# An attention and gated feed-forward block: a written-out opening, query heads parted by DMA, and a planner whose clocks wait for copies

## The chip, the cores and the metric

The kernel runs on one core of one Trainium2 chip. The metric is device time in microseconds (us). Nine runs of the kernel before lie between 734.39 and 735.54 us, with a median of 735.0 us.

The engines have short names in the profile: PE (TensorE matmul), PEld (TensorE weight load), DVE (VectorE), ACT (ScalarE), POOL (GpSimd) and SP (SyncE, which here only issues DMAs).

## What is computed

A block of a transformer over 2048 tokens of 512 features, with 32 heads of 16 features and a gated feed-forward part of 1792 features. All tensors are bfloat16.

```python
def _A_ref(x, wqkv, wo):
    qkv = (x @ wqkv).reshape(B, S, 3, H, Dh).transpose(2, 0, 3, 1, 4)
    q, k, v = qkv[0], qkv[1], qkv[2]
    scores = jnp.einsum("bhqd,bhkd->bhqk", q, k) * (Dh ** -0.5)
    o = jnp.einsum("bhqk,bhkd->bhqd", softmax(scores), v)
    return o.transpose(0, 2, 1, 3).reshape(B, S, D) @ wo

def _B_ref(x, w_gate, w_up, w_down):
    return (sigmoid(x @ w_gate) * (x @ w_up)) @ w_down

h = x + _A_ref(layernorm(x), A_wqkv, A_wo)
h2 = h + _B_ref(layernorm(h), B_w_gate, B_w_up, B_w_down)
```

## The kernel before, in words

**The main loop.** Scores are made transposed, 128 keys by 512 query columns at a time, for one head: 2048 such units in all. PE multiplies a slice of keys `KT` with queries `QT` (line 1110, 32 of its rows for each head) into a tile of PSUM that holds two or three units. ACT takes the exponential of most units (line 1475, into `pt` and into other buffers that are free at that time, so the profile shows the names `pe`, `xb`, `xnT` and `QTb` as well). DVE makes the exponential of the remaining units with integer arithmetic on 16-bit words (line 1292, tile `J`): one instruction writes the word, and two "chords", the same word plus a constant, are made by POOL as 64-bit integer additions (line 1313) or, early on, by DVE (line 1319). The three are summed in the product with the values: three matmuls for each such unit where an ACT unit has one. In a variant that the plan chooses ("both" in the code), DVE first adds two of the three as half-precision tiles (line 1337), which leaves two matmuls. PE multiplies probabilities with the values `Vaug` (line 1268), which carry a 17th column of halves, so that the sum of the probabilities comes out beside the output.

**Queries in pairs of groups.** The features of a 128-row projection hold eight heads of 16 rows. PE's scores read 32 rows at a time, so each projection goes into two tiles, `QT[2p]` and `QT[2p+1]`: one has the even heads and zeros in the rows of the odd ones, the other the reverse. In `prep_q` DVE scales the projection into `qd` (line 778), and `split_q` (line 327) multiplies `qd` with a mask column, once for each of the two tiles. This happens 15 times, for four blocks of 512 queries and four feature blocks, the first of them in the opening. One of the 15 goes to `QTb`, half of the tile `QTB`.

**Order.** Nothing is scheduled by the hardware or by a compiler: the Python program decides the order on each engine as it emits instructions. It keeps a clock for each engine, `T["P"]`, `T["A"]`, `T["D"]`, `T["G"]`, adds a fixed cost for every instruction, and places background work (projections, layer norms, the feed-forward part of finished query blocks) where these clocks have room. Jobs for DVE wait in the list `dq`, in order of priority. `need` (line 1090) forces the key and query jobs of a score unit to have been emitted before the scores. A table `PLAN`, with a number for a step of a score tile, overrides single decisions: how many value matmuls follow, whether a unit goes to DVE, whether PE rests, and others.

**The opening (lines 229 to 514).** SP and ACT's queue load the first 512 tokens, SP then the weights for the first feature block (`w0`), the other tokens and weights. POOL and DVE build an identity matrix from a ramp. For each of four token tiles, DVE or ACT makes mean and variance (ACT for the second tile), ACT the root, DVE the reciprocal (line 427) and the normalised tile `xn` (line 388), PE four transposes (line 308), ACT or DVE a copy out of PSUM (line 395). PE then projects keys and queries of the first feature block (line 401), and copies (lines 406 and 415) write the first parts of `KT` and `QT`. The order comes from a greedy list scheduler at lines 478 to 512 that takes the task with the best key of start and rank, with fixed costs, and keeps PE busy with filler matmuls (line 475). The scores begin when both halves of the query and the first half of the keys are there (`"go"`). The halves column of `Vaug` is written by ACT (line 265), the mask by DVE (lines 269 and 271), the accumulator is zeroed by DVE (line 514).

**After the opening.** `early_ln` normalises the other 1536 tokens (DVE statistics, POOL the rest), in blocks 2 and 3 with DMA transposes issued by SP (line 593). `prep_v` makes the values: a copy and a scaled copy on DVE (lines 323 and 324). `early_k` makes further keys of the first feature block (line 757), `prep_k` those of the others (line 767). In the feed-forward part SP issues transposes of the normalised `hn` (line 837), weight loads `wgu` with two buffers (line 855), loads of `x` (line 795) and stores (line 873). A filler matmul on `wo_sb` (line 678) keeps PE busy where nothing is ready.

Of the kernel before, what the change touches and what calls it, by code (L numbers as in the profile page):

```python
# [22 lines left out]
PLAN = {176: 5, 239: 2, 367: 1, 383: 1, 414: 3, 432: 9, 480: 5, 492: 1, 496: 3, 512: 4, 561: 1, 592: 3, 593: 9, 606: 3, 609: 3, 736: 5, 751: 2, 780: 2, 785: 1, 796: 1, 800: 4, 831: 1, 844: 2, 849: 3, 894: 3, 897: 9, 914: 9, 928: 3, 960: 2, 976: 3, 1025: 2, 1040: 3, 1041: 5, 1052: 2, 1072: 3, 1088: 2, 1100: 2, 1104: 5, 1105: 3, 1120: 3, 1170: 1, 1233: 3, 1280: 3, 1328: 4, 1359: 2, 1392: 3, 1440: 2, 1486: 3, 1681: 1, 1824: 5, 1840: 9, 1872: 4, 1953: 3, 1982: 1, 2001: 3, 2080: 3, 2095: 2, 2129: 3, 2161: 3, 2162: 2, 2176: 4, 2222: 1, 2239: 2, 2256: 4, 2257: 9, 2274: 4, 2287: 2, 2350: 3, 2412: 1, 2430: 2, 2465: 9, 2479: 2, 2480: 9, 2512: 2, 2556: 2, 2560: 4, 2574: 2, 2588: 2, 2592: 5, 2608: 9, 2767: 1, 2818: 3, 2833: 9, 2849: 5, 2864: 3, 2908: 1, 2972: 2, 3020: 1, 3036: 1, 3056: 1, 3072: 3, 3169: 4, 3180: 2, 3184: 4, 3217: 2, 3234: 4, 3280: 4, 3360: 2, 3537: 2, 3617: 3, 3644: 2, 3681: 9, 3744: 3, 3756: 2, 3760: 3, 3820: 2, 3905: 4, 3938: 3, 3953: 3, 4066: 4, 4080: 3, 4081: 4, 4096: 2, 4112: 2, 4124: 1, 4129: 9, 4191: 2, 4204: 1, 4207: 2, 4225: 3, 4268: 2, 4284: 1, 4288: 2, 4337: 2, 4352: 3, 4398: 3, 4510: 2, 4526: 1, 4641: 4, 4700: 2, 4734: 3, 4737: 4, 4752: 9, 4754: 2, 4784: 4, 4802: 4, 4878: 3, 4880: 4, 4910: 2, 4924: 1, 4928: 1, 4930: 4, 5022: 2, 5058: 3, 5072: 4, 5090: 3, 5121: 4, 5164: 1, 5182: 3, 5185: 3, 5200: 3, 5201: 3, 5265: 4, 5280: 3, 5294: 1, 5308: 1, 5345: 2, 5359: 1, 5360: 9, 5378: 3, 5388: 1, 5424: 1, 5471: 1, 5488: 1, 5522: 2, 5553: 3, 5566: 3, 5600: 2, 5633: 4, 5650: 9, 5696: 2, 5712: 4, 5728: 4, 5742: 2, 5756: 2, 5760: 3, 5840: 2, 5906: 1, 5938: 3, 6082: 9, 6095: 2, 6096: 2, 6108: 2, 6140: 1, 6192: 3, 6194: 9, 6268: 1, 6274: 3, 6289: 4, 6319: 1, 6337: 5, 6384: 1, 6431: 2, 6432: 4, 6463: 2, 6464: 4, 6528: 3, 6544: 3, 6592: 1, 6607: 2, 6624: 1, 6641: 2, 6656: 2, 6687: 2, 6689: 9, 6753: 9, 6799: 1, 6832: 2, 6847: 2, 6865: 1, 6929: 2, 6972: 2, 6974: 1, 7024: 1, 7040: 3, 7106: 9, 7152: 5, 7154: 9, 7244: 2, 7248: 3, 7281: 3, 7296: 2, 7312: 1, 7376: 2, 7408: 9, 7410: 2, 7468: 1, 7504: 4, 7505: 2, 7520: 3, 7535: 2, 7553: 4, 7566: 3, 7570: 4, 7585: 3, 7596: 2, 7676: 1, 7681: 5, 7695: 2, 7728: 4, 7776: 3, 7793: 2, 7839: 2, 7852: 1, 7886: 2, 8016: 2, 8033: 2, 8063: 2, 8128: 2, 8209: 4, 8257: 9, 8290: 4, 8305: 9, 8338: 4, 8382: 2, 8432: 5, 8494: 3, 8529: 5, 8591: 2, 8609: 5, 8626: 2, 8706: 3, 8721: 4, 8768: 4, 8800: 4, 8848: 2, 8849: 5, 8860: 1, 8863: 2, 8881: 3, 8882: 4, 8895: 2, 8896: 3, 8897: 2, 8910: 3, 8927: 1, 8946: 4, 8961: 4, 9006: 1, 9024: 3, 9026: 9, 9054: 3, 9073: 2, 9116: 2, 9120: 3, 9137: 4, 9153: 2, 9249: 5, 9276: 2, 9358: 2, 9376: 3, 9377: 9, 9407: 1, 9408: 1, 9426: 9, 9457: 3, 9504: 2, 9518: 3, 9520: 4, 9584: 9, 9586: 4, 9600: 2, 9678: 1, 9697: 1, 9711: 2, 9727: 2, 9728: 1, 9762: 9, 9776: 4, 9792: 4, 9841: 9, 9854: 2, 9855: 2, 9857: 9, 9872: 3, 9900: 1, 9919: 2, 9932: 1, 9964: 2, 9968: 3, 10028: 2, 10032: 2, 10044: 2, 10047: 1, 10146: 2, 10160: 5, 10172: 1, 10176: 3, 10177: 3, 10210: 4, 10273: 4, 10284: 1, 10304: 3, 10334: 1, 10364: 2, 10380: 2, 10417: 9, 10433: 4, 10464: 1, 10556: 1, 10622: 1, 10624: 4, 10626: 9, 10636: 1, 10640: 4, 10690: 3, 10702: 2, 10705: 3, 10734: 3, 10754: 4, 10801: 3, 10802: 2, 10816: 2, 10848: 9, 10912: 1, 10913: 1}  # L23
# [121 lines left out]
def kernel(  # L145
# [11 lines left out]
    nc = tc.nc  # L157
# [89 lines left out]
    nc.sync.dma_start(out=wo_sb[:], in_=A_wo.rearrange("(c p) n -> p c n", p=P))  # L247
# [8 lines left out]
    for k in range(32):  # L256
        nc.gpsimd.memset(ramp[:, 0, k:k + 1], float(k))
    nc.vector.memset(ident_bf[:], 0.0)
# [5 lines left out]
    def halves():  # L264
        nc.scalar.activation(out=Vaug[:, :, :, DH:VW], in_=fill[:].rearrange("p (t h o) -> p t h o", t=NT, o=1),
                             func=ACT.Copy, scale=0.5)

    def masks():
        nc.vector.tensor_reduce(out=mask[:], in_=ident_bf[:].rearrange("p (b a d) -> p a b d", a=2, d=DH),
                                axis=AX.XY, op=ALU.max)  # L270
        nc.vector.tensor_scalar(out=maskz[:], in0=mask[:], scalar1=ZS, scalar2=None, op0=ALU.mult)

# [57 lines left out]
    psp = main.enter_context(tc.tile_pool(name="psum", bufs=1, space=PSUM))  # L330
    PS = psp.tile([P, 8, QC], FP32, name="PS")
    free_banks = [5, 7, 6, 3, 2, 1, 0]
    held_banks = {}

    def bank0(key):
        b = held_banks[key] = free_banks.pop()
        return PS[:, b, :]

    def free0(key):
        free_banks.append(held_banks.pop(key))  # L340
# [7 lines left out]
    class Task:  # L348
        def __init__(self, name, deps, opts, bank=0, frees=0):
            self.name, self.deps, self.opts, self.bank, self.frees = name, deps, opts, bank, frees  # L350
            self.end = None
            tasks[name] = self

    def fixed(name, at):
        Task(name, [], []).end = at

    V, A, E = nc.vector, nc.scalar, nc.tensor

    ACT_STATS = {(0, 1)}

    def stats_task(c, i):
        src, mv = xb[c][:, i, :], mvs[c][:, i, :]

        def on_act():
            junk = work.tile([P, D], BF16, name="junk")
            A.activation(out=junk[:], in_=src, func=ACT.Identity, scale=1.0 / D,
                         accum_out=mv[:, 0:1])
            A.activation(out=junk[:], in_=src, func=ACT.Square, scale=D ** -0.5,
                         accum_out=mv[:, 1:2])
            buf["fix", c, i] = True  # L370
        Task(("s", c, i), [("x", c, i)], [("A", 1650, on_act)] if (c, i) in ACT_STATS
             else [("D", 870, lambda: ln_stats(src, mv))])
        Task(("f", c, i), [("s", c, i)], [("D", 300, lambda: fix(c, i))] if (c, i) in ACT_STATS
             else [("N", 0, lambda: None)])
# [19 lines left out]
    def copy0(c, i, eng):  # L394
        eng(out=xnv[c][:, i], in_=buf["t", c, i])
        free0(("t", i))
# [7 lines left out]
    def keys0(half, act):  # L404
        cs = slice(half * 2 * P, (half + 1) * 2 * P)
        (A.copy if act else V.tensor_copy)(out=KT[0][:, cs], in_=buf[0][:, cs])
        if half:
            free0(0)

    def query0(half, a, act=False):  # L410
        cs = slice(half * 2 * P, (half + 1) * 2 * P)
# [5 lines left out]
        if half and a:  # L417
            free0(1)

    fixed("w0", 5000.0)  # L420
    for c in range(NQC):
        for i in range(TQ):
            fixed(("x", c, i), (3150.0 + 450 * (i // 2)) if c == 0 else 4800.0 + 2100 * c + 150 * i)
            stats_task(c, i)
    for i in range(TQ):
        Task(("q", 0, i), [("f", 0, i)], [("A", 270, lambda i=i: root(i))])
        Task(("r", 0, i), [("q", 0, i)], [("D", 200, lambda i=i: V.reciprocal(
            out=rstds[0][:, i:i + 1], in_=rstds[0][:, i:i + 1]))])
        Task(("a", 0, i), [("r", 0, i)], [("D", 340, lambda i=i: apply(0, i))])
        Task(("t", 0, i), [("a", 0, i)], [("P", 400, lambda i=i: turn0(0, i))], bank=1)  # L430
        Task(("e", 0, i), [("t", 0, i)],
             [("A", 500, lambda i=i: copy0(0, i, A.copy)),
              ("D", 440, lambda i=i: copy0(0, i, V.tensor_copy))], frees=1)
        for w in (1, 0):
            Task(("p", w, i), [("e", 0, i), "w0"], [("P", 340, lambda w=w, i=i: proj0(w, i))], bank=int(i == 0))
    Task("mask", [("s", 0, 3)], [("D", 450, masks)])
    Task("halves", [("s", 0, 1)], [("A", 640, halves)])
    for h in range(2):
        for w in (1, 0):
            deps = [("p", w, 2 * h), ("p", w, 2 * h + 1)]  # L440
            if w:
                deps = deps + ["mask"]
                Task(("qt", h), deps, [("A", 450, lambda h=h: query0(h, 0, True)),
                                       ("D", 400, lambda h=h: query0(h, 0))])
                Task(("qu", h), deps, [("D", 400, lambda h=h: query0(h, 1))], frees=h)
            else:
                Task(("kt", h), deps, [("A", 410, lambda h=h: keys0(h, True)),
# [1261 lines left out]
```

## Time and profile before

| What | Value |
|---|---|
| median of nine runs | 735.0 us |
| the profiled execution | 734.96 us |
| its span | 733.2 us |
| DVE exponentials (line 1292) | 623, mean 679 ns |
| ACT exponentials into `pt` alone (line 1475) | 512, mean 1125 ns |
| sums of two tiles (line 1337) | 97, mean 702 ns |
| POOL chords (line 1313) | 658, mean 626 ns |
| projections of queries scaled, `qd` (line 778) | 15, mean 677 ns |
| granted TensorE clock | 0.999 of full speed |

A row of a timeline gives start and length in us, engine, line, operation, tile written and tile read, its shapes and the count, and in brackets how long the engine was idle before it and what ended that. A row of the waits gives who waited for whom, the total in us, how often and the longest. A group's row gives durations in ns as minimum, median and maximum. A busy engine is one with an instruction recorded on it; the records of neighbouring instructions overlap, so a short wait between two of them does not show as idle time.

### The profile page before, as it was taken

The numbers are of one execution on the slowest core, as the hardware profiler recorded it, in microseconds if no ns is written. First come the engines' busy times: TensorE is split into PE (matmuls) and PEld (weight loads), VectorE is DVE, ScalarE is ACT, GpSimd is POOL, SyncE is SP. The second block draws the span as 40 slices with busy tenths as digits, with TensorE's granted clock in tenths as the row PEclk, the third lists the DMA queues.
The fourth block names the chain that finished last, engine by engine and source line by source line (L and its number), as shares of the span: only waits on it lengthen the run. The fifth ranks groups of instructions, "written<-read, shape, count | busy, mean of one in ns | idle before, by whom it ended". The sixth has DMA issues, their size and how long they took to land.

```text
span 733.2 us, 26369 instructions
## 1 busy us (share of the span) xinstructions
PE 703.4 (96%) x11139; PEld 337.3 (46%) x11194; DVE 663.5 (90%) x1314; ACT 703.0 (96%) x787; POOL 421.7 (58%) x727
## 2 busy tenths in 40 slices
PE   7899999888999999999999999999999999999997
PEld 3222224443555445544545455445554455445564
DVE  6889999989999999999999899999999988999952
ACT  7999999999999999999999999999999999999962
POOL 2724667675665556656546656655654656656610
PEclk9999999999999999999999999999999999999999
DMA  7200005000223013220223023201322134012250
GB/s 244 51 9 2 1 1 175 2 3 2 74 75 88 10 27 101 84 56 25 59 67 86 20 69 101 66 25 31 101 61 52 38 89 117 17 44 80 84 175 18
DMA packets 80892, 44.49 MB, mean 61 GB/s; under 512 B 15488, under 2 KB 80768, under 8 KB 80768
## 3 DMA queue, kind: packets, MB, share of 16 engines
q1 hardware_dynamic: 80480, 42.48, 20.5%
q8 instruction: 89, 1.46, 0.9%
q14 instruction: 35, 0.29, 0.1%
q10 hardware_dynamic: 288, 0.26, 0.1%
HBM read 37.75 MB, written 2.10 MB: 54 GB/s over the span
## 4 chain that ended last, share of the span: by engine, by line
PE 48%; ACT 26%; DVE 18%; issue 4%; POOL 2%; DMA 1%; POOLq 0%; ACTq 0%; DVEq 0%
ACT pt L1475 18%; PE PS L1110 16%; PE PS L1268 13%; PE PS L847 8%; DVE J L1292 8%; PE PS L865 5%; ACT xnT L1475 3%; DVE J L1337 2%; POOL J L1313 2%; ACT th L877 2%; PE PS L319 1%; PE PS L314 1%; ACT QTb L1475 1%; DVE st L274 1%; ACT xb L1475 1%
## 5 line engine op out<-in xcount | busy, mean ns | idle before, releaser
L1313 POOL INT64_ADD J<-J x658 | 403.6, 626 | 260.9 <-DVE J L1292 211.2
L1475 ACT ACTIVATE pt<-PS 128x1024 f16<-128x1024 f32 (+1 forms) x512 | 512.9, 1125 | 3.9 <-PE PS L1110 2.8
L1292 DVE TENSOR_SCALAR J<-PS 128x512 int16<-128x512 f32 x623 | 411.4, 679 | 22.1 <-PE PS L1110 16.4
L1110 PE MATMUL PS<-QT,KT 32*128 32x256 bf16 (+1 forms) x3712 | 264.3, 276 | 15.0 <-ACT pt L1475 9.3
L1268 PE MATMUL PS<-J,Vaug 128*17 128x256 f16 (+1 forms) x3218 | 226.8, 279 | 0.9 <-DVE xs L1176 0.3
L1268 PE MATMUL PS<-pt,Vaug 128*17 128x256 f16 (+1 forms) x2021 | 191.8, 279 | 0.0
L1110 PEld LDWEIGHTS <-KT 32*128 32x128 bf16 x3840 | 90.3, 92 | 204.8 <-issue 201.2
L1268 PEld LDWEIGHTS <-Vaug 128*17 128x17 bf16 x5871 | 132.0, 90 | 79.8 <-issue 74.8
L847 PE MATMUL PS<-xnT,wgu 128*128 128x256 bf16 x784 | 112.5, 274 | 0.7 <-DVE qd L778 0.2
L1475 ACT ACTIVATE xnT<-PS 128x1024 f16<-128x1024 f32 (+1 forms) x88 | 96.1, 1128 | 0.0
L847 PEld LDWEIGHTS <-wgu 128*128 128x128 bf16 x784 | 64.4, 97 | 38.7 <-issue 33.0
L1337 DVE TENSOR_TENSOR J<-J 128x1024 f16<-128x1024 f16 (+1 forms) x97 | 67.9, 702 | 9.8 <-POOL J L1313 9.3
L865 PE MATMUL PS<-wd,hT 128*128 128x512 bf16 x169 | 51.0, 383 | 2.3 <-issue 2.2
L1268 PE MATMUL PS<-xnT,Vaug 128*17 128x256 f16 x360 | 51.8, 273 | 0.1
L877 ACT ACTIVATE th<-PS 128x512 f32<-128x512 f32 (+1 forms) x63 | 38.9, 618 | 8.4 <-DVE hT L860 5.6
L1475 ACT ACTIVATE QTb<-PS 128x1024 f16<-128x1024 f32 x39 | 43.1, 1105 | 0.3 <-PE PS L1110 0.3
L919 DVE SCALAR_TENSOR_TENSOR hT<-th,PS 128x512 bf16<-128x512 f32 x49 | 33.2, 678 | 2.8 <-PE PS L847 2.8
L1475 ACT ACTIVATE xb<-PS 128x1024 f16<-128x1024 f32 (+2 forms) x29 | 29.8, 1090 | 0.3 <-PE PS L1110 0.3
L1176 DVE STREAM_TRANSPOSE xs<-PS 128x256 f32<-128x256 f32 (+1 forms) x60 | 27.5, 458 | 1.8 <-PE PS L1268 1.6
L1475 ACT ACTIVATE pe<-PS 128x1024 f16<-128x1024 f32 (+2 forms) x26 | 25.9, 1059 | 1.7 <-PE PS L1110 1.6
L1268 PE MATMUL PS<-QTb,Vaug 128*17 128x256 f16 x156 | 27.1, 274 | 0.0
L1147 DVE TENSOR_TENSOR o<-xs,rsum 128x128 bf16<-128x128 f32 (+1 forms) x60 | 24.2, 404 | 2.1
(126 smaller groups left out, 394.0 us busy)
## 6 DMA issues: line engine op xcount, KB each, us to landing
wgu<-in_B_w_gate_dram SPq DMA_DIRECT2D x49, 256.0 KB, 3.0
wgu<-in_B_w_up_dram SPq DMA_DIRECT2D x49, 256.0 KB, 3.5
out_dram<-ob SPq DMA_DIRECT2D x16, 128.0 KB, 1.7
wd<-in_B_w_down_dram SPq DMA_DIRECT2D x1, 1792.0 KB, 8.8
xr<-in_A_x_dram SPq DMA_DIRECT2D x14, 128.0 KB, 3.5
xb<-in_A_x_dram SPq DMA_DIRECT2D x6, 256.0 KB, 6.0
J<-in_B_w_gate_dram SPq DMA_DIRECT2D x4, 384.0 KB, 5.3
J<-in_B_w_up_dram SPq DMA_DIRECT2D x4, 384.0 KB, 6.1
```

The costliest lines, as they stand in the source:

```text
L847: nc.tensor.matmul(ps[:, 0:PARTS[r][2]].rearrange("p (i q) -> p i q", q=P), lhsT=w[:, d, :], rhs=hn_of(r)[:, :, d, :], start=(d == 0), sto ...
L865: nc.tensor.matmul(ps, lhsT=hT[:, f, i * P:(i + 1) * P], rhs=wd[:, f, :], start=(f == 0), stop=(f == FC - 1))
L877: nc.scalar.activation(out=th[:, 0:ps.shape[-1]], in_=ps, func=ACT.Tanh, scale=0.5)
L919: nc.vector.scalar_tensor_tensor(out=hT[:, f:f + k, 0:w], in0=th[f][:].rearrange("p (k n) -> p k n", k=k), scalar=1.0, in1=ps2.rearrange(" ...
L1110: nc.tensor.matmul(pss[:, ui, i * CW[qc]:(i + 1) * CW[qc]], lhsT=KT[g // 2][32 * j:32 * j + 32, k * P:(k + 1) * P], rhs=q[32 * j:32 * j + ...
L1147: nc.vector.tensor_tensor(out=o2[:, 0:w // 32, DH * a:DH * a + DH], in0=xs[:, 0:w // 32, 0:DH], in1=rec.to_broadcast([P, w // 32, DH]), op ...
L1176: j = dve(650 - ns[0], lambda: nc.vector.transpose(out=xs[:, 0:w // 32, :].rearrange("p b r -> p (b r)"), in_=src), LAST, st["xs"], pr=-1)
L1268: nc.tensor.matmul(dst[32 * j:32 * j + VW, 0:w], lhsT=un.v[:, kt * SPAN[qc] + i, h, :], rhs=un.ap[:, i * w:(i + 1) * w], start=clears and ...
L1292: nc.vector.tensor_scalar(out=J[:, 0, k, :], in0=src, scalar1=ZOFF, scalar2=float(-min(CHORDS)), op0=ALU.add, op1=ALU.max)
L1313: nc.gpsimd.int64_add(words(s), words(0), CHORDS[s - 1] * (1 + 2 ** 16 + 2 ** 32 + 2 ** 48))
L1337: nc.vector.tensor_tensor(out=f1, in0=f1, in1=J[:, 0, 0:k, :].bitcast(FP16), op=ALU.add)
L1475: ex = nc.scalar.activation(out=pt, in_=pss[:, 0:wa, :], func=ACT.Exp, scale=AS)
```

## The change

1. The greedy scheduler of the opening, with its ranks, bank list and choices, is replaced by a fixed list of words `START`: an engine's letter (A, D, P) and a task's name, in the order in which they are emitted. Costs of tasks and the delay until another engine sees a result are new constants, used to place filler matmuls and to start the clocks. Banks of PSUM are fixed.
2. The halves of `Vaug`, zeros in `QTB` and the masks are made by DVE ahead of the first statistics; the zeroing of the accumulator goes from DVE to ACT (task `zero`).
3. The scores begin when the two halves of the first query tile, the first half of the keys and the exponential table are there. The second half of the keys and the second query tile (one instruction of 512 columns in place of two of 256) come behind the first scores.
4. SP copies the zeros of `QTB[:, 0]` to `QTB[:, 1]` and to the six other query tiles (seven DMAs of 128x512), and loads `wo_sb` only behind them.
5. `split_q` is no longer called in `prep_q`: once `qd` is written, SP issues eight DMAs of 16 rows each, alternately into the two query tiles, whose other rows stay zero. The planner books the queries 3300 ns after `qd`.
6. In the planner, `scores` waits with PE's clock for the key and query jobs, and value matmuls are only placed when the copy of their values is done by the clock (`values_in`). The time of a transpose by DMA is 4000 instead of 3000, and the pause at POOL's change of work 6000 instead of 9000.
7. `PLAN` is another table throughout.

```diff
-    def halves():
-        nc.scalar.activation(out=Vaug[:, :, :, DH:VW], in_=fill[:]..., func=ACT.Copy, scale=0.5)
+    nc.vector.memset(Vaug[:, :, :, DH:VW], 0.5)
+    nc.vector.memset(QTB[:], 0.0)
...
+    masks()
...
+START = "As1 Ds0 Ds2 Aq0 Dr0 Da0 Pt0 Aq2 Df1 Ds3 Aq1 Azero Ae0 Pp10 Dr2 Da2 Aq3 Aexps Dr1 Da1 Dr3 Da3 Pt2 De2 Pt1 Pp00 Pt3 Ae3 Pp12 De1 Pp01 Dkt0 Pp11 Dqt0 Pp13 Aqt1".split()
...
+    for word in START:
+        t, eng = tasks[word[1:]], word[0]
+        ns, fn = t.opts[eng]
+        at = max([free[eng]] + [seen(d, eng) for d in t.deps])
         if eng == "P":
-            keep_warm(start)
-            start = max(start, free["P"])
+            keep_warm(at)
+            at = max(at, free["P"])
+        t.end, t.eng = at + ns, eng
+        free[eng] = t.end
         fn()
-    acc = PS[:, 0, :]
-    nc.vector.memset(acc, 0.0)
+    go = max([free["P"]] + [seen(n, "P") for n in ("qt0", "qt1", "kt0", "exps")])
+    keep_warm(go)
+
+    for q in [QTB[:, 1, :]] + [q[:] for q in QT[2:]]:
+        nc.sync.dma_start(out=q, in_=QTB[:, 0, :])
+    nc.sync.dma_start(out=wo_sb[:], in_=A_wo.rearrange("(c p) n -> p c n", p=P))
...
-        job = pm_out(dve(603, lambda: nc.vector.tensor_scalar(
-            out=qd[:], in0=ps, scalar1=ZS, scalar2=None, op0=ALU.mult), st["mark"]))
-        done["q", qc, p] = [dve(262, lambda a=a: split_q(dst, a, qd), job) for a in range(2)]
+
+        def scale():
+            nc.vector.tensor_scalar(out=qd[:], in0=ps, scalar1=ZS, scalar2=None, op0=ALU.mult)
+            for k in range(2 * QC // 128):
+                rows = slice(DH * k, DH * k + DH)
+                nc.sync.dma_start(out=dst[k % 2][rows], in_=qd[rows])
+        job = pm_out(dve(603, scale, st["mark"]))
+        done["q", qc, p] = [Later(job, DMA_Q)]
...
+        T["P"] = max(T["P"], at + LAT)
         T["P"] = max(T["P"], ex_end.get(n - 2, 0.0) + LAT)
...
+    def values_in(un, loose):
+        if st["vin"]:
+            return True
+        end = After(("v", un.u[2] * SPAN[un.u[0]])).end
+        if un.u[0] < NCH and end is not None:
+            end = After(("v", NT - 1)).end
+            st["vin"] = end is not None and end + LAT <= T["P"]
+        return loose > 1e9 or end is not None and end + LAT <= T["P"] + loose
...
     pss_n = {0: scores(0)}
+    for i in (2, 3):
+        proj0(0, i)
+    pe_time("dense", 560.0)
+    query0(None, 1)
+    T["D"] = max(T["D"] + 660.0, T["P"] + DRAIN + LAT) + 430.0
+    keys0(1, False)
```

In the task names, s is statistics, f their repair where ACT made them, q the root, r the reciprocal, a the normalised tile, t the transposes, e the copy out of PSUM, p10 the query projection of token tile 0 and p00 that of its keys, qt0 and qt1 the two halves of the first query tile, kt0 the first half of the keys; the digit behind the other letters is the token tile.

## The prediction

> **What bounds the kernel now.** I read the page's parts 1 and 4 first, then the table of stages, the waits of 25 to 50 us, and the opening's timeline. The profiled execution spans 733.2 us and took 734.96 us, so 1.76 us lie around the span; the median of the nine runs is 735.0, so no correction is needed between the two. A measurement of this kernel can tell about 0.2% (1.5 us) from no change.
>
> ```profile
> PE 703.4 (96%) x11139; PEld 337.3 (46%) x11194; DVE 663.5 (90%) x1314; ACT 703.0 (96%) x787; POOL 421.7 (58%) x727
> PE 48%; ACT 26%; DVE 18%; issue 4%; POOL 2%; DMA 1%; POOLq 0%; ACTq 0%; DVEq 0%
> 13.20:25.00 11.80, 10.72 (x73) 3.62 (x74) 11.28 (x28) 11.56 (x13) 6.93 (x14) 1.00 0.26 81
> 25.00:50.00 25.00, 23.54 (x136) 6.77 (x136) 21.08 (x44) 22.44 (x25) 11.28 (x21) 1.00 0.22 43
> 50.00:110.00 60.00, 59.65 (x573) 16.18 (x572) 57.14 (x99) 59.70 (x64) 36.26 (x60) 1.00 0.01 1
> 110.00:690.00 580.00, 562.14 (x9924) 281.85 (x9969) 544.40 (x1065) 577.07 (x634) 359.01 (x584) 1.00 0.21 60
> ```
>
> The stage rows give length, then busy us of PE, PEld, DVE, ACT, POOL, then granted clock (1.00 throughout). PE and ACT are both nearly full from 13.2 to 690 us and share the chain of waits. Three places are left: the opening up to the first exponential (13.2 us), the stage of 25 to 50 us (ACT busy only 22.44 of 25), and the long middle, where work itself must shrink. The middle is less full than its 577 busy us say: exponentials of 1024 columns follow each other every 0.906 us when fed (ten between 15.36 and 24.42 us), while their records last 1.125, so waits under 0.2 us don't show. The last 33 us (700 on) hold the output's tail, which the change leaves as it is.
>
> ```profile
> ACT pe L1475 <- PE PS L1110: 1.6, 3, 0.7
> PE PS L1110 <- DVE KT L757: 1.1, 1, 1.1
> ACT pt L1475 <- PE PS L1110: 0.9, 2, 0.6
> ```
>
> These are the waits of 25 to 50 us (total, times, longest): ACT waits 2.5 us for scores, and PE 1.1 us for one key copy on VectorE.
>
> **The opening's new order.**
>
> ```profile
> 0.85 0.11 DVE L258 MEMSET ident_bf<- 128x64 uint32 x1
> 2.41 0.21 DVE L259 STREAM_TRANSPOSE ramp<-ramp 128x32 bf16<-128x32 bf16 x1 [1.45 <-POOL ramp L257]
> 3.58 0.69 DVE L274 BATCH_NORM_STATS2 st<-xb 128x6 f32<-128x512 bf16 x1 [0.22 <-DMA xb<-in_A_x_dram]
> 8.79 0.61 PE L308 MATMUL PS<-ident_bf,xn 128*128 128x128 bf16 x8 [0.76 <-DVE mask L269]
> 10.18 2.38 ACT L265 ACTIVATE Vaug<-fill 128x512 bf16<-128x512 bf16 x1
> 11.80 0.83 PE L401 MATMUL PS<-xnT,w 128*128 128x128 bf16 x12 [0.64 <-DVE QT L415]
> 12.76 0.40 PE L1110 MATMUL PS<-QT,KT 32*128 32x512 bf16 x4
> 13.19 1.94 ACT L1475 ACTIVATE pt<-PS 128x1024 f16<-128x1024 f32 x2
> ```
>
> Before, three token tiles are measured in a row and all four normalised late (first xn at 6.87 us), ACT spends 2.38 us on the halves column of Vaug, PE waits 0.64 us for a query copy in the bank that it must write, and the first scores start at 12.76. The new order interleaves the tiles. With this trace's durations I place it step by step.
>
> The two new VectorE memsets (Vaug's halves, QTB) are not in the trace; the nearest row is the 128x512 memset of the accumulator, 0.48 us. Two of them run from 0.96 to about 2.0, under the 1.45 us that VectorE waits for the ramp: cost nothing; without that cover, 1 us. The masks (0.28 + 0.17 us), moved up, follow the identity's end at 3.36, so statistics start at about 3.87 instead of 3.58. Tile 0 ends at 4.8, tile 2 at 5.6; ACT's statistics of tile 1 end at 5.26 as before, its root of tile 0 (0.28) fits, and tile 0 is normalised at 6.1 (reciprocal 0.14, apply 0.40). Its four transposes (0.40) end at 6.55, and the ACT copy (0.57), behind two roots and the zeroing of the accumulator (0.6 by the same copies, the planner puts 1 ns), at 7.7. Tile 3 is normalised at 8.5, and its transposes end at 9.1. VectorE copies tiles 2 and 1 until 9.33 (0.42 each). ACT loads its exponential table from 7.95 to 9.45 (1.28 + 0.20) and then copies tile 3 until 10.04. Projections of four matmuls take 0.38: keys of tile 1 until 9.76, the key copy (0.42) until 10.2, the first query half (0.48) until 10.7. The last projection must wait for that copy, as at 11.80 above, and ends at 11.1; ACT's query half (0.40) ends at 11.55. First scores at about 11.65, first exponential at 12.1: **1.1 us earlier**. If one ACT or VectorE step meets its neighbour badly, 0.6; if the model is right everywhere, 1.4. The second half of the keys goes behind the first scores: eight more projection matmuls (0.6 us) lie between score tiles 0 and 1, under the first exponential's 0.906, so they are hidden; VectorE gets to the next statistics at 12.9 instead of 13.99, which lets the early stage move along with the opening.
>
> **SP's queue in the opening.** Seven zero copies (128 KB each) stand ahead of wo. Loads in that stretch are issued every 0.4 to 1.3 us; wo was issued at 8.40 and landed after 8.6 us, and can now land some 4 to 7 us later. Its first reader was a filler matmul at 23.2 us; in the built order of the changed kernel the first such filler stands behind 800 matmuls, so nothing waits. Without the cover: 0 to 1 us.
>
> **Queries parted by DMA.**
>
> ```profile
> L327 DVE TENSOR_SCALAR QT<-qd,mask x28: 312/346/739, 67.1 to 562.5; 128x512 bf16<-128x512 bf16 x28
> L873 SPq DMA_DIRECT2D out_dram<-ob x14: 356/357/362, 247.6 to 710.3; - x14
> DMA to landing us min/median/max: 1.7/1.7/2.6
> DVE J L1337 <- POOL J L1313: 9.3, 20, 1.4
> ```
>
> Thirty mask multiplications leave VectorE: 28 x 0.421 (their mean) + 2 x 0.344 = 12.5 us. In their place SP issues 15 groups of eight DMAs of 16 rows. [...] The row has 0.36 us per issue and 1.7 us to land for 128 KB, so eight in flight give 8 x 0.36 + 1.7 to 2.6 = 4.6 to 5.5 us; I take 5, nearest to a row. The tightest user is the first one: its query was scaled at 52.84 us and first read by a score at 66.94. [...] The others lie further apart. [...]
>
> Each group also delays what stands behind it on SP, weight loads, transposes of hn and output stores, by 8 x 0.36 = 2.9 us, and an entry waits for the transfer eight places ahead of it, so up to 2.6 more. Weight loads have two buffers, and SP already waits 287 us for PE to release them: hidden, and at most one pair late. Price: 0 to 0.4 us for each of the eleven groups that lie among the feed-forward work, 0 taken.
>
> **What the freed VectorE does.** The built order has 14 more wide sums of two probability tiles and one narrow one less (+14 x 0.745 - 0.44 = 10.0 us), 3 more exponentials (+3 x 0.679 = 2.0 us), two chords less (-0.5). VectorE ends even. The sums save second passes of values: 18 matmuls of 256 columns and 12 of 512 fewer, 42 units of 256; forty take 1.21 us, so PE saves 1.3 us. Three more filler matmuls, at most 3 x 0.38 = 1.1, are put where PE would idle. ACT has three 1024-column exponentials turned into 512: 3 x 0.45 = 1.4 us less. Both limiting engines so shrink by 0.2 to 1.4 us; with the new plan's order unknown, half of it, **0.7 us**, and a bound of -2 to +2 for the order (some 15 us of short ACT waits in the middle, moved by a tenth or so). Every added sum waits for GpSimd: 9.3 us over 97 before, 0.1 each, so 1.4 us more on VectorE, which idles 36 us there (580 - 544).
>
> **Clocks that wait for copies.** No instruction is added. Scores are booked behind the key and query copy, values behind theirs, so the order offers PE other work where it stood 1.1 us for a key copy. Of ACT's 2.5 us in 25 to 50 us I take **1.0** as recovered; 0 if VectorE is simply behind, 2.5 if all goes.
>
> Sum: 735.0 - 1.1 - 1.0 - 0.7 = **732.2 us**.
>
> **Rivals.** *The faster one:* all early waits go (2.5), the opening gives 1.4, the limiting engines the full 1.4: 735.0 - 5.3 = 729.7. For it: the early stage's losses all stem from order. Against: its copies still need VectorE, 21 to 23 of 25 us busy.
>
> *It doesn't do what it says:* the first exponential starts earlier, but the early stage is paced by statistics, value and key copies and PE, so ACT idles later by as much, and the new plan gives nothing: 735.0 less 0.2, 734.8. For it: PE at 59.65 of 60 us from 50 to 110. Against: VectorE's start moves along.
>
> *The slower one:* SP's in-order queue. A group of eight stands ahead of a transpose of hn, whose 3.23 us to land is already once in the chain (at 649.5), and PE's feed-forward matmuls then wait for hn or weights. It decides once the eleven groups cost PE more than (2.8 + 1.5) / 11 = 0.39 us each; at 0.7 each it is 732.2 + 7.7 = 739.9. For it: 2.9 to 5.5 us of delay per group. Against: before, PE waits for that transfer for 0.2 us in all, and loads are prefetched.
>
> **How the numbers follow.** Likeliest, 732.2 (731 to 733.4): 0.50. The faster one: 0.22. No change: 0.16. The slower one: 0.12. The first two are faster by over 0.2%: 0.72. The range, 729.0 to 735.8, takes in both bounds of the early waits and of the plan's order and leaves out the slower rival and a little of the faster one.
>
> **What would show it.** Right: first scores near 11.65 us, first exponential near 12.1; ACT's waits in 25 to 50 us near 1.5; no wait of PE on a query DMA; SP issues of the parting DMAs at 0.36 to 0.45 us; VectorE's busy time within 3 us of 663; ACT and PE about 1 us less busy. Wrong: PE waiting for hn or weights, sums waiting longer than 0.1 us each on GpSimd, an early stage as long as the opening is short, or more ACT waits in 110 to 690 us.

## The result and the profile after

The changed kernel takes 732.41 us (median of nine runs, 731.87 to 733.27) against 734.93 us for the kernel before on the same chip: a ratio of 0.9966, with a 95% interval of 0.9958 to 0.9974. It is faster by 0.34%, 2.5 us. The profiled execution took 732.01 us with a span of 730.1 us, some 3.0 us less than the 733.2 us of before (before rounding).

From the page of the changed kernel, busy time and the chain of waits by engine; below them, from its table of stages, the rows of 25 us on (columns as in the prediction):

```profile
PE 703.5 (96%) x11111; PEld 335.8 (46%) x11169; DVE 664.6 (91%) x1299; ACT 700.1 (96%) x786; POOL 426.4 (58%) x728
PE 64%; ACT 24%; DVE 7%; issue 4%; DMA 1%; POOL 1%; SPq 0%; DVEq 0%; ACTq 0%; POOLq 0%
```

```profile
25.00:50.00 25.00, 23.60 (x139) 6.84 (x140) 21.54 (x43) 23.44 (x26) 12.69 (x24) 1.00 0.22 43
50.00:110.00 60.00, 58.25 (x559) 16.33 (x560) 56.34 (x96) 59.02 (x62) 33.41 (x54) 1.00 0.04 9
110.00:690.00 580.00, 564.11 (x9938) 281.39 (x9988) 547.59 (x1059) 578.22 (x637) 365.16 (x591) 1.00 0.23 62
```

ACT is fuller by 1.0 us from 25 to 50 us and emptier by 0.7 from 50 to 110, where PE also loses 1.4. In the middle it is fuller by 1.15. The totals don't show the change: PE's stays (703.4 us before), VectorE's rises by 1.1, and ACT's falls by 2.9, of which 2.38 is the write of the halves column that left ACT. The chain has more of PE and less of DVE (18% before, 7% now).

The timeline of the opening in the changed kernel:

```profile
2.58 0.48 DVE L263 MEMSET Vaug<- 128x512 bf16 x1 [1.72 <-issue]
3.10 0.48 DVE L264 MEMSET QTb<- 128x512 uint32 x1
3.58 0.15 DVE L266 STREAM_TRANSPOSE ramp<-ramp 128x32 bf16<-128x32 bf16 x1
4.91 0.69 DVE L279 BATCH_NORM_STATS2 st<-xb 128x6 f32<-128x512 bf16 x1
11.74 0.40 PE L395 MATMUL PS<-xnT,w 128*128 128x128 bf16 x4 [0.69 <-DVE QT L407]
12.71 0.39 PE L1061 MATMUL PS<-QT,KT 32*128 32x512 bf16 x2
13.14 3.77 ACT L1442 ACTIVATE pt<-PS 128x1024 f16<-128x1024 f32 x4 [0.50 <-PE PS L1061]
```

The first scores start at 12.71 us (12.76 before), the first exponential at 13.14 (13.19). The new opening is shorter from the first statistics on (8.2 us against 9.6), but its statistics start at 4.91 instead of 3.58 us: the memset of `Vaug` stands at 2.58 us, with 1.72 us of idle VectorE ahead of it that is put down to "issue", and the ramp's transpose comes only behind the memset of `QTB`, at 3.58 instead of 2.41.

The waits that answer to those of before, in the changed kernel (the first two from 25 to 50 us; the others from 110 to 690), and the row of the parting DMAs with their landing:

```profile
ACT pt L1442 <- PE PS L1061: 0.9, 3, 0.4
ACT xb L1442 <- issue: 0.5, 1, 0.5
```

```profile
DVE J L1298 <- POOL J L1274: 12.0, 22, 1.3
PE PS L1061 <- DMA QT<-qd: 0.5, 1, 0.5
```

```profile
L728 SPq DMA_DIRECT2D QT<-qd x112: 507/587/1595, 70.1 to 559.7; - x112
DMA to landing us min/median/max: 1.7/1.8/3.6
```

**A ledger.** Busy time hides short waits (in the changed kernel the record of a 1024-column exponential into `pt` lasts 1.093 us in the mean, while the next one starts after 0.904 us when it is fed), so I use the distances from one ACT instruction's start to the next. Their tenth percentile, over the traces of before and after, is what an exponential costs when it is fed: 1.330 us for 1536 columns, 0.904 for 1024, 0.477 for 512. Between the first exponential and the last one of 1024 columns or more, the sum of these is ACT's work, and what is left of the time is its waits. With the start of the first exponential and what follows the start of the last, this adds up to the span. All runs below are in this table:

| kernel | first exponential | ACT's work | ACT's waits | behind | span |
|---|---|---|---|---|---|
| before | 13.19 | 665.18 | 20.02 | 34.8 | 733.2 |
| after | 13.14 | 663.42 | 19.09 | 34.5 | 730.1 |
| e1 parting on VectorE | 13.14 | 663.42 | 28.99 | 35.0 | 740.6 |
| e2 parting DMAs twice | 13.14 | 663.42 | 44.84 | 34.7 | 756.1 |
| e3 memsets later | 12.02 | 663.42 | 19.69 | 34.9 | 730.1 |
| e4 memsets, masks later | 11.95 | 663.42 | 20.92 | 34.6 | 730.9 |
| e9 memsets swapped | 13.10 | 663.42 | 19.13 | 35.1 | 730.7 |
| e10 memsets on GpSimd | 12.15 | 663.42 | 18.60 | 34.3 | 728.5 |
| e5 before, no table | 13.35 | 663.90 | 32.71 | 35.6 | 745.5 |
| e6 after, no table | 13.13 | 665.17 | 33.30 | 34.7 | 746.3 |
| e7 e6 without clock waits | 13.13 | 667.73 | 33.98 | 33.9 | 748.7 |
| e8 before, table of after | 13.28 | 671.57 | 35.67 | 35.6 | 756.1 |
| e11 e6, parting on VectorE | 13.14 | 666.03 | 33.32 | 35.7 | 748.2 |
| e12 after, one entry less | 13.13 | 671.14 | 34.33 | 34.4 | 753.0 |

From before to after: opening -0.05, work -1.76 (three exponentials of 1024 columns less, two of 512 more), waits -0.93, behind -0.3: together -3.0. What stands behind the last wide exponential moves by as much between executions of one and the same order (34.3 to 35.1 us in the rows of after, e3, e4, e9 and e10, whose work is the same), so it is not counted as a gain; and the profiled execution is 0.4 us faster than the median of the nine. One narrow exponential (0.48) now stands behind the last wide one, so the work fell by about 1.3 in all. The waits by stage (to 50, to 110, to 300, to 500 us, to the end) were 3.97, 1.86, 4.60, 4.86, 4.73 and are 2.81, 2.66, 5.30, 3.40, 4.93: 1.2 us won early, 1.5 lost again by 300 us, 1.5 won once more from 300 to 500.

So the total came out as predicted, and its parts did not. My theory was that the memset of `Vaug`, whose elements lie apart from each other in memory (a strided write), had cancelled the opening, and that the rest came from the work that leaves VectorE. The rivals: GpSimd or the start of the engine held VectorE; and, for the rest, that the new table is a better one whatever else changes.

### The profile page after: what moved, and what is told of

Read it like the earlier page. It is cut to its first block, busy times and chain, and to the rows that moved or that the text cites. A ratio compares the mean times of both kernels' runs of the same rounds, so it can differ in the third digit from the quotient of the medians.

```text
span 730.1 us, 26491 instructions
## 1 busy us (share of the span) xinstructions
PE 703.5 (96%) x11111; PEld 335.8 (46%) x11169; DVE 664.6 (91%) x1299; ACT 700.1 (96%) x786; POOL 426.4 (58%) x728
## 4 chain that ended last, share of the span: by engine, by line
PE 64%; ACT 24%; DVE 7%; issue 4%; DMA 1%; POOL 1%; SPq 0%; DVEq 0%; ACTq 0%; POOLq 0%
PE PS L1061 21%; PE PS L1229 18%; ACT pt L1442 17%; PE PS L797 11%; PE PS L815 5%; DVE J L1253 3%; PE PS L319 3%; ACT xnT L1442 3%; PE PS L324 2%; ACT QTb L1442 1%; PE PS L740 1%; ACT th L827 1%; ACT xb L1442 1%; PE PS L1636 1%; POOL J L1274 1%
## 5 line engine op out<-in xcount | busy, mean ns | idle before, releaser
L1274 POOL INT64_ADD J<-J x658 | 407.9, 632 | 253.9 <-DVE J L1253 205.0
L1442 ACT ACTIVATE pt<-PS 128x1024 f16<-128x1024 f32 (+2 forms) x523 | 519.6, 1112 | 2.8 <-PE PS L1061 2.2
L1061 PE MATMUL PS<-QT,KT 32*128 32x256 bf16 (+1 forms) x3712 | 263.9, 276 | 13.7 <-ACT pt L1442 5.6
L1229 PE MATMUL PS<-pt,Vaug 128*17 128x256 f16 (+1 forms) x2042 | 198.4, 279 | 0.0
L1442 ACT ACTIVATE xnT<-PS 128x1024 f16<-128x1024 f32 (+1 forms) x85 | 92.1, 1114 | 0.5 <-PE PS L1061 0.2
L1298 DVE TENSOR_TENSOR J<-J 128x1024 f16<-128x1024 f16 (+1 forms) x110 | 78.5, 714 | 12.8 <-POOL J L1274 12.0
L1229 PE MATMUL PS<-xnT,Vaug 128*17 128x256 f16 x346 | 46.7, 274 | 0.0
L1442 ACT ACTIVATE xb<-PS 128x1024 f16<-128x1024 f32 (+1 forms) x25 | 26.0, 1084 | 0.6 <-issue 0.5
L1442 ACT ACTIVATE pe<-PS 128x1024 f16<-128x1024 f32 (+1 forms) x21 | 21.8, 1093 | 0.9 <-PE PS L1061 0.8
```

Source lines behind the costliest of these rows:

```text
L1061: nc.tensor.matmul(pss[:, ui, i * CW[qc]:(i + 1) * CW[qc]], lhsT=KT[g // 2][32 * j:32 * j + 32, k * P:(k + 1) * P], rhs=q[32 * j:32 * j + ...
L1229: nc.tensor.matmul(dst[32 * j:32 * j + VW, 0:w], lhsT=un.v[:, kt * SPAN[qc] + i, h, :], rhs=un.ap[:, i * w:(i + 1) * w], start=clears and ...
L1274: nc.gpsimd.int64_add(words(s), words(0), CHORDS[s - 1] * (1 + 2 ** 16 + 2 ** 32 + 2 ** 48))
L1298: nc.vector.tensor_tensor(out=f1, in0=f1, in1=J[:, 0, 0:k, :].bitcast(FP16), op=ALU.add)
L1442: ex = nc.scalar.activation(out=pt, in_=pss[:, 0:wa, :], func=ACT.Exp, scale=AS)
```

## The experiments

Ratios are to the kernel before on the same chip, whose median was 735.2 to 735.4 us in all of them.

**e1: the parting back on VectorE, everything else as in the changed kernel.** The planner's order stays exactly as it was, so the 30 multiplications are not booked.

```diff
-            for k in range(2 * QC // 128):
-                rows = slice(DH * k, DH * k + DH)
-                nc.sync.dma_start(out=dst[k % 2][rows], in_=qd[rows])
+            for a in range(2):
+                nc.vector.tensor_scalar(out=dst[a][:], in0=qd[:], scalar1=mask[:, a:a + 1], ...)
```

> The changed kernel with the query heads parted by two mask multiplications on VectorE again, emitted right behind the scaling, and nothing else moved: the planner's clocks and so the order of all other instructions stay. Theory 1 (the freed VectorE is what shortens the middle): 12.5 us of VectorE work come back, of which about a fifth, VectorE's share of the chain before, ends on the path: 734.5 to 735.5 us, ratio to before about 1.000. Theory 2 (the new order and its smaller PE and ACT work shorten the middle; VectorE idles there anyhow): 732.0 to 733.0 us, ratio 0.997.

742.15 us, ratio 1.0092 [1.0076, 1.0107]: by the two ratios 9.3 us slower than the changed kernel, more than either theory had. VectorE's busy time rises from 664.6 to 676.0 us, and ACT's waits by 9.9 us with the same work (the ledger). The engines of this run:

```profile
PE 710.8 (96%) x11111; PEld 338.0 (46%) x11169; DVE 676.0 (91%) x1329; ACT 703.7 (95%) x786; POOL 428.1 (58%) x728
```

So of 11.4 us that go back onto VectorE in an order without room for them, most reach the end. It shows that VectorE's time is scarce in this order; it does not show what an order made for those multiplications would lose.

**e2: each parting DMA followed by a copy of itself**, of the same 16 rows into a tile that nobody reads.

```diff
                 nc.sync.dma_start(out=dst[k % 2][rows], in_=qd[rows])
+                nc.sync.dma_start(out=spare_q[rows], in_=qd[rows])
```

> The changed kernel with each of the 120 parting DMAs followed by a second one of the same size into a tile that nobody reads: 240 issues on SP, the double price of the queue. If SP's in-order queue already costs something (weight loads or hn transposes late by 8 x 0.59 us per group), doubling adds at least as much again: 733.5 us or more. If it is hidden: 732.4 within 0.7 us, though PE's one wait for a query DMA (0.5 + 0.8 us in the changed kernel) can grow to some 3 us.

757.48 us, ratio 1.0299 [1.0283, 1.0314]. The waits of this run from 110 to 690 us, and its row of 200 to 300 us:

```profile
ACT pt L1444 <- PE PS L1063: 20.0, 13, 5.2
PE PS L799 <- DMA wgu<-in_B_w_gate_dram: 13.3, 4, 4.8
PE PS L1063 <- DMA QT<-qd: 4.3, 1, 4.3
```

```profile
200.00:300.00 100.00, 93.85 (x1608) 46.41 (x1614) 89.96 (x172) 93.53 (x104) 59.95 (x98) 0.97 0.24 68
```

PE stands 13.3 us for feed-forward weights, in four waits of up to 4.8 us, and once 4.3 us for a query; ACT's waits grow by 25.8 us. In the changed kernel only one wait of 0.5 us has such a cause. The weights come late because they are issued late: from issue to landing the loads of `w_gate` take 3.1 us in the median, 3.0 in the changed kernel. This is the mechanism of the slower rival. With 120 of these DMAs it costs nothing that shows, with 240 it costs 25 us; no load in between was run. The granted clock is 0.97 in each 100 us from 200 to 600, 1.00 in the changed kernel: its records have four stretches of 6.83 us at 0.50, one behind each of the four longest stalls (3.2 to 4.8 us), so a part of these 25 us may be a slower PE behind its stalls; how much was not measured (as an estimate from these records, at most 4 x 6.83 x 0.50 = 13.7 us).

**e3: both memsets behind the opening's tasks.**

```diff
-    nc.vector.memset(Vaug[:, :, :, DH:VW], 0.5)
-    nc.vector.memset(QTB[:], 0.0)
...
     for word in START:
...
+    nc.vector.memset(Vaug[:, :, :, DH:VW], 0.5)
+    nc.vector.memset(QTB[:], 0.0)
```

> The changed kernel with VectorE's two new memsets (Vaug's halves and QTB) moved behind the last VectorE step of the opening's list, in front of the second query tile. Theory: in the changed kernel they started at 2.58 instead of 0.86 us and pushed the first statistics to 4.91; without them statistics start at about 3.9 and the first scores at 11.7 instead of 12.71, the first exponential at 12.1 to 12.3. If the early stage follows the opening, 731.4 us (1.0 less); rival: the stage of 25 to 110 us is paced by its own work, and 732.2 to 732.6 us come out although the first exponential is 1 us earlier.

732.10 us, ratio 0.9957 [0.9944, 0.9971]. The first scores start at 11.59, the first exponential at 12.02, 1.1 us earlier than in the changed kernel and where the prediction had them. But VectorE now pays in the early stage. Its timeline there:

```profile
10.08 0.47 DVE L405 TENSOR_SCALAR QT<-PS,maskz 128x256 bf16<-128x256 f32 x1
12.25 0.48 DVE L456 MEMSET Vaug<- 128x512 bf16 x1 [1.69 <-issue]
12.76 0.48 DVE L457 MEMSET QTb<- 128x512 uint32 x1
```

The same gap, 1.69 us, stands ahead of the same memset ten microseconds later, when GpSimd had only one instruction of 0.26 us (at 10.91 us) between 2.4 and 15.8 us. The next statistics on VectorE, ahead of other tokens, start at 14.04 us, as in the changed kernel (14.03), although the scores started 1.1 us earlier. Of the 1.12 us, ACT's waits take back 0.60, all of it before 50 us (3.47 us against 2.81), and the rest is lost in the part behind the last wide exponential, which scatters by as much. The ratio differs from that of the changed kernel by less than the intervals can tell.

**e4: as e3, and the masks built behind the copy of tile 1** instead of ahead of the statistics.

```diff
-    masks()
...
+        if word == "De1":
+            masks()
```

> As the run with the late memsets, and the masks (0.29 + 0.17 us on VectorE) too go from ahead of the first statistics to behind the copy of token tile 1, where VectorE waited 0.47 us. First statistics at 3.5 (then bound by the arrival of the first tokens), first exponential at 11.8 to 12.2 us. If the opening counts in full, 731.0 us; if not, 732.2 to 732.6.

731.68 us, ratio 0.9952 [0.9938, 0.9965]; first exponential 11.95, another 0.07 us. The profiled execution is the slowest of the five (732.71 us), with ACT's waits 1.2 us above e3's, all from 110 us on. The masks were not what the opening had lost.

**e9: the two memsets of the changed kernel in the other order.**

```diff
-    nc.vector.memset(Vaug[:, :, :, DH:VW], 0.5)
     nc.vector.memset(QTB[:], 0.0)
+    nc.vector.memset(Vaug[:, :, :, DH:VW], 0.5)
```

> The changed kernel with the two VectorE memsets in the other order: the contiguous one of QTb first, the strided one of Vaug second. If the 1.7 us ahead of Vaug's record is the price of its strided two-byte write itself, QTb starts at about 0.86 us and Vaug's record still has about 1.7 us of idle ahead of it (it ends at about 3.5 us; first statistics still at about 4.9). If something else holds VectorE until 2.58 us (GpSimd's work, or a start of the engine), QTb starts at 2.58 and Vaug follows at once at 3.1. The whole stays at 731.5 to 732.5 us by either.

One run, 732.52 us. The timeline of VectorE:

```profile
0.94 0.48 DVE L263 MEMSET QTb<- 128x512 uint32 x1
3.12 0.48 DVE L264 MEMSET Vaug<- 128x512 bf16 x1 [1.70 <-issue]
4.87 0.69 DVE L279 BATCH_NORM_STATS2 st<-xb 128x6 f32<-128x512 bf16 x1
```

VectorE was free at 0.94 us and wrote the contiguous tile in 0.48; the gap goes with the strided one. So the memset of 512 single two-byte elements per partition, 34 bytes apart, takes 1.70 + 0.48 = 2.2 us, and its record covers only the last 0.48. The rival (something holds VectorE until 2.58 us) is out.

**e10: both memsets on GpSimd, ahead of its instruction that brings 8 us of "issue" with it, and the masks as in e4.**

```diff
-    nc.gpsimd.tensor_scalar(out=eps4_t[:], in0=eps4_t[:], ...)
...
-    nc.vector.memset(Vaug[:, :, :, DH:VW], 0.5)
-    nc.vector.memset(QTB[:], 0.0)
+    nc.gpsimd.memset(Vaug[:, :, :, DH:VW], 0.5)
+    nc.gpsimd.memset(QTB[:], 0.0)
+    nc.gpsimd.tensor_scalar(out=eps4_t[:], in0=eps4_t[:], ...)
```

> The changed kernel with both memsets on GpSimd, ahead of nothing that the opening waits for, and the query masks built behind the first group of opening tasks. If the memsets are the whole of what the opening lost, first scores at about 11.5 and first exponential at about 11.9 us, and, since VectorE is also spared 2.7 us near 10.6 to 13.2 us that moving them later had cost, 731.2 to 731.7 us. [...]

Twelve runs in two heaps: eight from 730.34 to 732.11 us (median 731.2) with a granted clock of 0.998 to 1.000 over the run, and four from 737.16 to 738.39 us with 0.989 to 0.993. Over all twelve the median is 731.9 and the ratio 0.9979 [0.9956, 1.0003], so this is no sure gain. The profiled run is of the first heap, and its fastest; the timeline of GpSimd in it, and the row of VectorE's next statistics:

```profile
2.31 2.28 POOL L262 MEMSET Vaug<- 128x512 bf16 x1
4.18 1.26 POOL L263 MEMSET QTb<- 128x1024 bf16 x1
15.39 0.38 POOL L532 TENSOR_SCALAR nv<-mv 128x2 f32<-128x2 f32 x1
```

```profile
13.04 0.68 DVE L277 BATCH_NORM_STATS2 st<-xb 128x6 f32<-128x512 bf16 x1
```

The record of the strided write has 2.28 us here (the next instruction starts 1.87 us after it, so the two records overlap by 0.41), while 1024 contiguous elements of the same type take 1.26. So it is the stride and not the type here. Nothing waits for it: GpSimd's first work for the token tiles starts at 15.39 us, in the changed kernel at 15.81. The first exponential starts at 12.15 instead of 13.14, VectorE's statistics move along (13.04 instead of 14.03), and this time nothing is given back: ACT's waits are 0.5 us lower as well, and the last wide exponential is 1.5 us earlier. In this execution the opening's microsecond reaches the end. What slowed the clock in the four other runs is open, since none of them left a trace, and it may come from this very change: the 17 runs of the kernel before on this chip lie within 1.2 us of each other. As an estimate, 10 us at a clock of 0.50 (e8, below, has one stretch of 10.24) would take 0.007 off the mean clock of 735 us, about what they lack.

**e5 and e6: both kernels with an empty table; e7: e6 without the clocks' waits; e8: the kernel before with the table of the changed one.**

```diff
-PLAN = {64: 3, 128: 1, ...
+PLAN = {}
```

```diff
-        T["P"] = max(T["P"], at + LAT)
...
-                and un.end + LAT <= T["P"] + loose and values_in(un, loose)]
+                and un.end + LAT <= T["P"] + loose]
```

> The kernel before with an empty PLAN, so that every decision is the planner's own rule. With the next two it tells how much of the gain is the structure (opening, DMA parting, clocks) and how much the table. Slower than before by 1 to 3% in any case. If the structure makes the gain, the changed kernel without a plan is faster than this one by 2 us or more; if the table makes it, the two are within 1 us or in the other order.

> The changed kernel with an empty PLAN. Structure theory: 2 us or more faster than the kernel before with an empty PLAN. Table theory: within 1 us of it, or slower; then the 2.6 us of the whole change are the fit of the new table.

> The changed kernel with an empty PLAN and without its two clock waits: scores don't wait by PE's clock for key and query copies, and values are placed without asking for their copy. If the waits help by themselves, this is 1 us or more slower than the same kernel with them, with longer waits of PE for KT copies before 50 us; if not, within 0.7 us.

> The kernel before with the PLAN table of the changed kernel, which was not made for its steps. If a table is worth something only with the code that it was made for, this is as slow as the kernel before with an empty PLAN, or slower (1 to 3% over before); if the new table simply asks for better choices (more sums), 733 to 735 us.

Without a table the kernel before takes 747.60 us (ratio 1.0168 [1.0150, 1.0186]), the changed one 748.42 (1.0181 [1.0163, 1.0200]): the change's parts earn nothing there. Leaving out the clocks' waits as well gives 750.35 us (1.0199 [1.0181, 1.0217]), 1.9 us more (the intervals overlap, the single runs do not). The ledger by stage has 0.5 us more of ACT's waits up to 50 us, where the step of the prediction had put it, and 1.4 more from 50 to 110; behind that the two orders part (5.4 less to 300 us, 4.0 more from there to 500). Over the whole, ACT's waits differ by 0.7 us only and its work by 2.6, so the 1.9 us are not the waits that the clocks save early. The kernel before with the other's table takes 757.75 us (1.0332 [1.0275, 1.0389]), worse than with none. Each table is worth 12 to 16 us to its own code, and the one that was tried on the other's is a loss there. The reverse, the changed kernel with the table of before, was not tried, nor were the two changed constants of the planner (4000 and 6000) alone.

**e11: e6 with the parting on VectorE, this time booked by the planner.**

```diff
-            for k in range(2 * QC // 128):
-                rows = slice(DH * k, DH * k + DH)
-                nc.sync.dma_start(out=dst[k % 2][rows], in_=qd[rows])
...
-        done["q", qc, p] = [Later(job, DMA_Q)]
+        done["q", qc, p] = [dve(262, lambda a=a: split_q(dst, a, qd), job) for a in range(2)]
```

> The changed kernel without its table and with the parting of the heads booked again on VectorE as two multiplications of 0.36 us a group (no parting by DMA), beside 748.4 us for the changed kernel without its table. If the freed VectorE is worth something by itself, whatever order a table gives, this run is slower than 748.4 by 2 to 9 us: 750.5 to 757. If it is worth something only to a table fitted to it, 747.5 to 749.

751.25 us, ratio 1.0227 [1.0212, 1.0241], against 1.0181 [1.0163, 1.0200] for e6: 0.46%, 3.4 us, in the range that the freed VectorE was to show. The planner makes 87 wide sums here and 91 in e6. But ACT's work differs by 0.9 us only, and its waits not at all; of the 1.9 us between the two profiled executions 1.0 stand behind the last wide exponential. So I don't take the 3.4 us as its price.

**e12: one entry of the changed kernel's table left out** (`545: 9`, an early decision on value matmuls).

> The changed kernel with one entry of its table of 400 left out (545: 9, an early one). If the table's value is a fit of the whole order, one entry left out shifts all that is chosen behind it and costs several microseconds: 735 to 745 us. If the gain comes from the parts of the change and the table only polishes, it stays within 1 us: 731.5 to 733.5.

754.23 us, ratio 1.0258 [1.0244, 1.0273]: far outside both expectations. The table has 326 entries, not the 400 of the expectation. With one gone, the order is another one from there on, and the later entries, made for the old one, no longer serve it: ACT's work rises by 7.7 us (fewer exponentials are given to VectorE, 609 against 626), its waits by 15.2, and the table is worse than none. Of this, 9.6 us are lost between the thousandth and the 1200th score unit (76.7 us instead of 67.1), and most of that in one place; PE's wait there, and some of the stages of 2 us around it in this run:

```profile
PE PS L1229 <- DVE J L1298: 3.0, 1, 3.0
```

```profile
388.00:390.00 2.00, 0.00 (x0) 0.00 (x0) 1.86 (x7) 0.00 (x0) 0.00 (x0) 0.90 0.17 37
390.00:392.00 2.00, 1.74 (x20) 0.90 (x19) 0.81 (x2) 0.59 (x1) 0.00 (x0) 0.50 0.11 29
394.00:396.00 2.00, 2.00 (x30) 1.10 (x23) 0.45 (x1) 0.00 (x0) 0.00 (x0) 0.50 0.93 60
398.00:400.00 2.00, 1.98 (x28) 1.06 (x28) 1.49 (x4) 2.00 (x3) 1.36 (x3) 1.00 0.01 4
```

PE waits 3.0 us for one wide sum of VectorE, and the records of the clock then have 6.83 us at 0.50, from 389.6 us on.

## Why the prediction was right and wrong

The sum (-2.8 us) was met (-2.5 by the medians, -3.0 by the spans), and the time lay well inside the range. That the sum came out is in part luck: the opening missed its 1.1 us, and the order of the later blocks, for which only a bound of 2 us either way had been given, won about as much. By its steps:

- **The opening, -1.1: wrong, -0.05.** The failed step is "Two of them run from 0.96 to about 2.0, under the 1.45 us that VectorE waits for the ramp: cost nothing". The nearest row was a contiguous memset (0.48 us); one of the two is strided and takes 2.2 us (e9, e3). The two ended at 3.58 us instead of 2.0, and the statistics came 1.3 us later than in the kernel before. A nearer row had been shown in the same fence: ACT's write of the same column, 2.38 us. I had taken that for ACT's slowness, and VectorE needs about as long for the same column (2.2 us, e9). The rest of the opening holds: without the memsets the statistics start at 3.79 us (predicted 3.87), the first scores at 11.59 (11.65) and the first exponential at 12.02 (12.1). Moving them later doesn't yet win the microsecond, since VectorE then lacks it (e3).
- **The clocks that wait for copies, -1.0: right in its place, not at the end, and the cause is open.** ACT's waits from 25 to 50 us fell from 2.5 to 1.4, and PE's wait for a key copy from 1.1 to 0.5. But the kernel gave 1.5 us back between 50 and 300 us, as the "doesn't do what it says" rival had it; why is not shown, as the orders differ. Without tables, the clocks change 0.5 us up to 50 us (e7 against e6), and the changed kernel has 4.00 us of waits there against 4.05 for the kernel before (e6, e5): half of the early gain or more may be the new table's.
- **The middle, -0.7: right in kind, too small.** I had worked out 1.4 us less work for ACT and taken half of it, the order being unknown. The work fell by 1.3 in all, by 1.76 ahead of the last wide exponential, and the order won another 1.2 us of waits from 300 us on (within the bound of 2). PE's busy time, for which I had 1.3 us less, did not fall (703.4 to 703.5 us).
- **The tail, left as it is: -0.3**, no more than its scatter.
- **The parting by DMA, 0: right, with too small an issue and the wrong tightest user.** SP needs 0.587 us for each, not the 0.36 of an output store: a group takes 8 x 0.587 + 1.8 = 6.5 us instead of 5. The first group, taken for the tightest, had its 14 us. But the group issued from 267.26 us on was wanted by PE some 6 us later, and that is the one wait of 0.5 us (e2: 4.3 us in the same place). "The others lie further apart" was wrong; that it cost so little was luck. PE never waited for weights or for `hn`. That an entry on SP waits for the transfer eight places ahead of it shows in the opening of the changed kernel: the last zero copy started at 14.46 us and the load of `wo_sb` at 15.97, each after SP had stood 1.0 us until `wq_sb` and `wk_sb`, eight issues ahead of them, had landed.
- **The slower rival: the mechanism exists, the load doesn't reach it.** Doubling the DMAs sets it off (e2: PE waits 13.3 us for weights).
- **Waits of the sums for GpSimd**: 0.1 us each predicted, 12.0 / 110 = 0.11.

What is shown of the middle's gain is this: the changed order has 97 wide sums instead of 83 and three exponentials of 1024 columns less on ACT; it breaks by some 9 us when VectorE gets its multiplications back (e1); and the same parts without a table gain nothing (e5, e6). So the gain is one of the order that the new table makes. That the table found it because VectorE was freed fits all this but is argued, not shown: an order made for the kernel before might have found as much, and how much is open. A single entry is worth some 20 us (e12), so pairs of kernels without tables, as in e5 to e7 and e11, differ by the luck of an order as well, and the few microseconds between them can't be put down to one part.

## What to carry to other kernels

Price an instruction by the row that has its access pattern, not by its name and element count: for a write that took 2.2 us, the same column written by another engine (2.38 us) was a better measure than a contiguous memset on the right one (0.48). Where an order has been fitted offline to a program, no part of the program can be judged by leaving it out of that order; count what the order does (work, waits, by stage) and compare that. A microsecond won ahead of a full stage was kept here only where what was moved did not fall to an engine that this stage needs (e10 against e3).

## What the runs showed of the hardware

- **Single two-byte elements, 34 bytes apart, cost about the same on three engines**: 2.2 us on VectorE (e9), 2.38 on ACT (the kernel before), 2.28 on GpSimd (e10; 1.87 by the start of its next instruction) for 512 of them in each partition, about 4 ns each. Contiguous ones took 0.48 us for 512 words of four bytes on VectorE and 1.26 us for 1024 of two bytes on GpSimd, 0.9 and 1.2 ns each. No other stride was run, and what in the access costs the time is not shown.
- **The profile shows such a write on VectorE as idle time.** VectorE's record has only the last 0.48 us; the 1.72, 1.69 and 1.70 us ahead of it (the changed kernel, e3, e9) are printed as "issue", while GpSimd's record has the whole 2.28.
- **Behind stalls of PE the granted clock was 0.50 for some microseconds.** Six pauses without a matmul, of 3.0 to 4.8 us (four in e2, one each in e6 and e12), were each followed by a stretch at a granted clock of 0.50; one of 1.6 us (e2) was not. Two more such stretches (e7, e8) came behind shorter pauses close together, with PE busy for 0.72 and 0.59 of 2 us just ahead. All eight (the last 10 us of each run left out) lasted 3.41 us (e6, e7), 6.83 (e2, e12) or 10.24 (e8); the mean granted clock of these runs was 0.998 (e6, e7), 0.98 (e2), 0.994 (e12) and 0.993 (e8). How long a pause has to be, and what sets the length of a stretch, is not shown.
- **An issue of a DMA of 16 rows between two tiles on the chip took SP 0.587 us in the median (0.507 to 1.595)**, where a store of an output tile takes 0.357. It is not the small number of rows: six copies of 128 rows between two tiles (the zeros) took 0.568 us in the median.
